# Top-k attention and a gated network on one core: bounds and epsilon moved from ScalarE to VectorE

## The chip, the core and the metric

The kernel runs on one core of a Trainium2 chip. Its time is the device time of one execution in microseconds (us); a kernel's time is the median of its runs. The core has five engines that run side by side and wait for each other through semaphores: TensorE (PE; its weight loads are listed as PEld), VectorE (DVE), ScalarE (ACT), GpSimd (POOL) and SyncE (SP), which here only issues transfers. [...]

## The reference, cut to what matters

Two stages follow each other. First attention over 8 batches of 8 heads with 576 positions of 64 values, in which each row keeps only its 32 largest scores; then a network with a gate on the 4608 x 512 result.

```python
scores = scale * np.matmul(q, k.transpose(0, 1, 3, 2))        # scale = 1/8
kth = np.partition(scores, -top_k, axis=-1)[..., -top_k:-top_k + 1]   # top_k = 32
mask = scores >= kth
scores = np.where(mask, scores, -1000000000.0)
scores = scores - np.max(scores, axis=-1, keepdims=True)
attn = np.exp(scores)
attn = attn / (np.sum(attn, axis=-1, keepdims=True) + 1e-09)
x = np.matmul(attn, v)          # then (B,H,S,D) -> (B*S, H*D) = 4608 x 512
h = x @ w_in                    # 512 x 2048
g = h * np.cos(h)
return g @ w_out                # 2048 x 512
```

Two numbers per row are needed between the scores and the exponential: the 32nd largest score, for the mask, and the largest, for the shift. They are called the bounds here. The epsilon is the 1e-09 that is added to the row's sum. The weights w_in and w_out arrive as 64-bit floats and are put together from two 32-bit words each on the core.

## The kernel before, in words

**Units and slots.** A unit is one pair of heads for one block of 128 tokens; there are 36 blocks times 4 pairs, 144 units. The main loop (L853) goes through slots. In slot i VectorE searches the largest scores of unit `u` = i, ScalarE masks and exponentiates unit `w` = i - 1, GpSimd packs unit `x` = i - 2 for the transpose, and TensorE, in every even slot, multiplies the two units `z` (i - 4 and i - 3) by the values. Between these pieces `feed` places matmuls of the network: `ff1` (L497, h) and `ff2` (L572, the output). There are three kinds of slots: `early_slot` for the first nine (i up to EARLY = 8), where weights are still loaded and transposes are done by TensorE; `slot` for the 132 in the middle (9 to 140), where the weights go through GpSimd's packing and a transposing transfer; and `last_slot`. In some of the middle slots (the first ones) weights are still decoded. All orders are written out by hand in these three functions; no scheduler changes them.

**The search on folded halves.** The 576 scores of a row are folded into two halves of 288: `rest` holds the larger of each pair (`fold_high`, L242, VectorE, one input in PSUM, the matmuls' accumulator memory, and one in SBUF, the main on-chip memory), `low` the lesser. The lesser is made on GpSimd as sum minus larger, on integers: `fold_sum` (L252) and then `fold_low` (L261). `low` has one buffer, so L252 of a unit waits until VectorE has ended the last search on the `low` of the unit before. The searches themselves are rounds of MAX8 (L323) and MATCH_REPLACE8 (L326), four rounds on `rest` and two on `low`. `merge_first` (L311) and `merge_second` (L316) join both lists to the 32nd largest; they run one slot later, around that slot's L242.

**Bounds, mask, exponential.** `bounds` turns the two ends of the list into `nb` (both times -1/8; L333) and, for each of the two heads, `nd` (the difference of the two bounds; L336), on ScalarE. `mask` (L345) and `exponentials` (L353), also on ScalarE, use them; the exponential also leaves the row sums in `den`, to which L358 adds the epsilon. `reciprocal` (L362, VectorE) follows at the head of the next slot.

**GpSimd in a middle slot.** In order: L252 (`fold_sum` of u), L379 and L381 (`split`: the words of x and its reciprocal in halves for the transfer), L261 (`fold_low`), then parts of the network: the gate's product (L559), or conversion and difference (L533, L542).

**VectorE in a middle slot.** In order: reciprocal L362, L311, L242, L316, all searches, and in even slots at the end two products that scale the values (`scale_values`, L451, two inputs in SBUF); these stand just ahead of the next slot's reciprocal.

**Weights.** `decode_first` (ScalarE) turns the high words into floats (L130) and rounds the low words to integers (L133); `decode_second` (VectorE) shifts the high part (L141); `decode_third` (GpSimd) adds the two (L151). 32 chunks of 128 x 512 go this way.

Of the kernel before, what the change touches and what calls it, by code (L numbers as in the profile page):

```python
# [10 lines left out]
F32 = mybir.dt.float32  # L11
I32 = mybir.dt.int32
U32 = mybir.dt.uint32
U16 = mybir.dt.uint16
AF = mybir.ActivationFunctionType
ALU = mybir.AluOpType

P = 128
TOPK = 32
NEG = -3.4028234663852886e38  # L20
EPS = 1e-9
# [9 lines left out]
def kernel(  # L31
# [9 lines left out]
    nc = tc.nc  # L41
    ctx.enter_context(tc.manual_schedule())
    B, H, D, S = qT.shape
# [6 lines left out]
    HS = S // 2  # L50
    SCALE = 1.0 / math.sqrt(D)
# [3 lines left out]
    consts = ctx.enter_context(tc.tile_pool(name="consts", bufs=1))  # L55
# [10 lines left out]
    nc.vector.memset(halfpi, math.pi / 2.0)  # L66
    quarter = consts.tile([P, 1], F32, tag="quarter")
    nc.vector.memset(quarter, 0.25)
    eps = consts.tile([P, 1], F32, tag="eps")
    nc.vector.memset(eps, EPS)  # L70

# [50 lines left out]
    def decode_first(n):  # L124


        for _ in range(min(n, len(wq["loaded"]))):
            st, w = wq["loaded"].popleft()
            lo, hi = st[:, :, 0], st[:, :, 1]
            nc.scalar.activation(  # L130
                out=w, in_=hi.bitcast(F32), func=AF.Prelu, scale=2.0**-111, alpha=2.0**32
            )
            nc.scalar.mul(out=lo, in_=lo.bitcast(U32), mul=2.0**-29)  # L133
            wq["second"].append((st, w))

    def decode_second(n):

        for _ in range(min(n, len(wq["second"]))):
            st, w = wq["second"].popleft()
            wi = w.bitcast(I32)  # L140
            nc.vector.tensor_scalar(  # L141
                out=wi, in0=wi, scalar1=3, scalar2=None, op0=ALU.logical_shift_left
            )
            wq["third"].append((st, w))
# [92 lines left out]

    def fold_high(u):

        s, sc = u["s"], u.pop("sc")  # L240
        u["rest"] = work.tile([P, 2, S], F32, tag="rest", name="rest", bufs=1)
        nc.vector.tensor_tensor(  # L242
            out=u["rest"][:, :, HS:S], in0=sc[:, :, 0:HS], in1=s[:, :, HS:S], op=ALU.max
        )

    def fold_sum(u):

        if not u["folds"]:
            return
        s = u["s"].bitcast(I32)  # L250
        u["low"] = work.tile([P, 2, HS], F32, tag="low", name="low", bufs=1)
        nc.gpsimd.tensor_tensor(  # L252
            out=u["low"].bitcast(I32), in0=s[:, :, 0:HS], in1=s[:, :, HS:S], op=ALU.add
        )

    def fold_low(u):

        if not u["folds"]:
            return
        low = u["low"].bitcast(I32)  # L260
        nc.gpsimd.tensor_tensor(  # L261
            out=low, in0=low, in1=u["rest"][:, :, HS:S].bitcast(I32), op=ALU.subtract
        )
# [9 lines left out]
    def topk_first(u, w):  # L273

        u["top"] = tops[u["n"] % len(tops)]
        merges = w and w["folds"]
        if merges:
            merge_first(w)
        if u["folds"]:
            fold_sum(u)  # L280
            fold_high(u)
            if u["n"] <= EARLY:
                fold_low(u)
        else:
            u["rest"] = work.tile([P, 2, S], F32, tag="rest", name="rest", bufs=1)
        if merges:
            merge_second(w)
        topk_round(u, 0)

    def topk_round(u, rnd):  # L290
# [24 lines left out]
    def merge_second(u):  # L315
        nc.vector.tensor_reduce(  # L316
            out=u["top"][:, :, TOPK - 1, 1], in_=u.pop("lesser"), axis=mybir.AxisListType.X,
            op=ALU.max,
        )
# [8 lines left out]
    def bounds(u):  # L328

        ends = u.pop("top").rearrange("p j r i -> p j (r i)")  # L330
        ends = ends[:, :, 2 * TOPK - 2 :] if u["folds"] else ends[:, :, 2 * TOPK - 2 :: 2 - 2 * TOPK]
        nb = u["nb"] = small.tile([P, 2, 2], F32, tag="nb", name="nb")
        nc.scalar.mul(out=nb, in_=ends, mul=-SCALE)  # L333
        nd = u["nd"] = small.tile([P, 2], F32, tag="nd", name="nd")
        for j in range(2):
            nc.scalar.activation(  # L336
                out=nd[:, j : j + 1], in_=ends[:, j, 1:2], func=AF.Identity,
                bias=nb[:, j, 0:1], scale=SCALE,
            )

    def mask(u):

# [6 lines left out]
    def exponentials(u):  # L349
        s, nd = u["s"], u.pop("nd")  # L350
        den = u["den"] = small.tile([P, 2], F32, tag="den", name="den")
        for j in range(2):
            nc.scalar.activation(  # L353
                out=s[:, j], in_=s[:, j], func=AF.Exp, bias=nd[:, j : j + 1], scale=1.0,
                accum_out=den[:, j : j + 1],
            )

        nc.scalar.activation(out=den, in_=den, func=AF.Identity, bias=eps, scale=1.0)  # L358

    def reciprocal(u):  # L360
        u["rden"] = small.tile([P, 2], F32, tag="rden", name="rden")
        nc.vector.reciprocal(u["rden"], u.pop("den"))  # L362

    def normalise(u):
        s, rden = u["s"], u.pop("rden")
# [266 lines left out]
    EARLY, LAST = 2 * NP, NU - NP  # L632
# [26 lines left out]
    def early_slot(i, u, w):  # L659
        n = 3 if i < 6 else 2  # L660
        topk_first(u, w)
        if i == 0:
            decode_second(1)
        scores(units[i + 1])
        for load, b, hp in at_slot.get(i, []):
            load(b, hp)
        load_weights(n)
        if w:
            bounds(w)
            mask(w)  # L670
            exponentials(w)
        topk_round(u, 1)

        decode_second(n)
        if w:
            reciprocal(w)
        topk_round(u, 2)
        topk_round(u, 3)
        if w:
            normalise(w)  # L680
        take_banks()
        take_scores(units[i + 1])
        gate(1)
        decode_third()
        feed(2)
        reduce_first()
        reduce_second()
        if i != NP:
            decode_first(n - 1)
        if w:  # L690
            transposes_now(w)
        feed(1)
        decode_first(n - len(wq["second"]))
        if w:
            values([w])
            take_values([w])
        feed(2)
        sines(2)
# [7 lines left out]
    def slot(i, u, w, x, z):  # L706
        if x:
            reciprocal(x)
        if u:
            topk_first(u, w)  # L710
            decode_second(2)
        if x:
            send(x)
        if u:
            fold_low(u)
            topk_round(u, 1)
            topk_round(u, 2)
            topk_round(u, 3)
        made = scored.get(i, [])
        if z:  # L720
            take_banks()
        feed(1)

        ahead = i < EARLY + 5 * NP
        if z and not ahead:
            values(z)
        for m in made:
            scores(m)
        if z and ahead:
            values(z)  # L730


        late = len(made) > 0

        decoding = i < EARLY + 8
        if i % 2 and not decoding:
            sines(1)
        if w:
            bounds(w)
            mask(w)  # L740
        take_banks()
        if w and late:
            exponentials(w)
        if z and not ahead:
            take_values(z)
        take_scores(units[i + 1])
        if z and ahead:
            take_values(z)
        if z:
            scale_values(z)  # L750
        if w and not late:
            exponentials(w)
        load_weights(2)
        for load, b, hp in at_slot.get(i, []):
            load(b, hp)
        gate(1)
        feed(1 if len(made) == 2 else 2)
        take_banks()
        decode_third()
        decode_first(2)  # L760
        reduce_first()
        reduce_second()
        feed(1 if len(made) == 2 else 3)
        if decoding or i == LAST:
            sines(1)

    def last_slot(i, u, w, x, z):
        if x:
            reciprocal(x)
        if u:  # L770
            topk_first(u, w)
            fold_low(u)
            topk_round(u, 1)
        bounds(w)
        mask(w)
        exponentials(w)
        take_banks()
        sines(1)
        if z:
            values(z)  # L780
        if i + 1 < NU:
            scores(units[i + 1])
        if z:
            take_values(z)
            scale_values(z)
        if i + 1 < NU:
            take_scores(units[i + 1])
        if x:
            send(x)
        reciprocal(w)  # L790
        normalise(w)
        if u:
            topk_round(u, 2)
            topk_round(u, 3)
        gate(2)
        feed(2)
        transposes_now(w)
        take_banks()
        reduce_first()
        reduce_second()  # L800
        feed(1)
        values([w])
        take_values([w])
        feed(2)
# [71 lines left out]
```

## Time and profile before

| | |
|---|---|
| time, median of 3 runs | 1498.96 us (1487.91 to 1499.81) |
| span of the profiled run | 1491.0 us |
| TensorE busy | 1409.2 us, 95% of the span |
| VectorE busy | 1332.0 us, 89% |
| ScalarE busy | 1217.2 us, 82% |
| GpSimd busy | 1165.1 us, 78% |
| `nb` L333, x144 | 199 ns each |
| `nd` L336, x288 | 287 ns each |
| epsilon L358, x144 | 296 ns each |
| low words L133, x32 | 679 ns each |
| L252 and L261, x142 each | 1439 and 1417 ns each |
| L379, x132 | 2107 ns each |

Busy time is the time in which an engine had at least one instruction in work; overlapping instructions of one engine count once. A row of the timeline gives start and duration in us from the span's start, the engine, the line, the operation, output and inputs; in brackets stands how long the engine was idle before it and what ended that wait. The chain of waits is followed back from the last instruction to what released each one, and says which engine's work the end of the kernel hangs on. The table by stages gives the busy time of each engine in a stretch, with the number of instructions in parentheses.

### The profile page before, as it was taken

To read this page: it belongs to the slowest core of one execution; us is meant where nothing else is said; L and a number is where in the kernel's file an instruction comes from. 1 tells how busy PE (TensorE), PEld (TensorE's weight loads), DVE (VectorE), ACT (ScalarE), POOL (GpSimd) and SP (SyncE) were. 2 spreads that over 40 slices of the span, in tenths; PEclk is the share of its full clock that TensorE was granted. 3 is DMA by queue.
4 is the path that set the end of the run, shared out by engine and by line. 5 is a ranking of instruction groups with operands and counts; after the bars stand their busy time and mean duration, and the time that the engine had idled before them with its cause. 6 is when DMAs were issued, how large, how long until landed. Compare 5 with 4: busy or idle time off the path is not lost.

```text
span 1491.0 us, 30595 instructions
## 1 busy us (share of the span) xinstructions
PE 1409.2 (95%) x10360; PEld 1013.3 (68%) x10360; DVE 1332.0 (89%) x4764; ACT 1217.2 (82%) x2438; POOL 1165.1 (78%) x822
## 2 busy tenths in 40 slices
PE   5678599999999999999999999999999999999998
PEld 3456366777777777777767777677667777777665
DVE  6888899999999999999999999999999999999721
ACT  6887778888888888888888888888888888888651
POOL 5688777888888888888888888888888888888410
PEclk9888799999999999999999999999999999999999
DMA  8523476656665566556655566656765566555200
GB/s 265 159 86 101 138 203 160 156 146 187 190 165 149 149 176 192 160 151 193 180 165 149 149 179 175 171 149 160 198 170 146 149 165 181 160 147 148 70 8 15
DMA packets 405549, 229.54 MB, mean 154 GB/s; under 512 B 355088, under 2 KB 371728, under 8 KB 405392
## 3 DMA queue, kind: packets, MB, share of 16 engines
q1 hardware_dynamic: 399984, 217.93, 53.8%
q10 hardware_dynamic: 5408, 9.65, 1.8%
q8 instruction: 82, 1.34, 0.4%
q14 instruction: 75, 0.61, 0.1%
HBM read 45.09 MB, written 95.94 MB: 95 GB/s over the span
## 4 chain that ended last, share of the span: by engine, by line
PE 76%; ACT 12%; DVE 5%; DMA 4%; issue 1%; POOL 0%; SPq 0%; ACTq 0%; POOLq 0%
PE mm L497 29%; PE o L572 28%; PE rim L432 10%; PE sc L223 7%; DMA pT<-rows 2%; ACT s L353 2%; DVE top L323 2%; PE rim L223 2%; ACT s L345 2%; ACT s L233 1%; DVE rest L326 1%; ACT L353 1%; ACT L552 1%; ACT x L552 1%; DVE xT L451 1%
## 5 line engine op out<-in xcount | busy, mean ns | idle before, releaser
L497 PEld LDWEIGHTS mm<-xT,w_in 128*128 128x128 f32 x4608 | 538.2, 192 | 74.5 <-issue 51.4
L572 PE MATMUL o<-w_out,g 128*128 128x512 f32 x1152 | 540.4, 603 | 17.2 <-POOL w_out L151 13.6
L497 PE MATMUL mm<-xT,w_in 128*128 128x128 f32 x4608 | 542.1, 276 | 6.2 <-DVE xT L451 2.8
L323 DVE MAX8 top<-rest 128x8 f32<-128x288 f32 x1148 | 470.3, 451 | 0.0
L326 DVE MATCH_REPLACE8 rest<-top,rest 128x288 f32<-128x288 f32 (+1 forms) x860 | 376.3, 445 | 0.0
L252 POOL TENSOR_TENSOR low<-s 128x576 int32<-128x576 int32 x142 | 204.4, 1439 | 197.5 <-DVE top L323 81.1
L572 PEld LDWEIGHTS o<-w_out,g 128*128 128x128 f32 x1152 | 203.1, 191 | 205.0 <-issue 181.3
L379 POOL COPY halves<-s 128x2304 uint16<-128x2304 uint16 x132 | 278.1, 2107 | 0.5 <-DMA rows<-halves 0.5
L353 ACT ACTIVATE s<-s,nd 128x576 f32<-128x576 f32 x288 | 220.3, 766 | 14.0 <-ACT ob L582 13.2
L323 DVE MAX8 top<-low 128x8 f32<-128x288 f32 x568 | 229.1, 445 | 0.0
L345 ACT ACTIVATE s<-s,nb 128x576 f32<-128x576 f32 x288 | 205.3, 760 | 0.0
L261 POOL TENSOR_TENSOR low<-low,rest 128x576 int32<-128x576 int32 x142 | 201.2, 1417 | 1.8 <-DVE top L316 0.9
L432 PEld LDWEIGHTS rim<-pT,v 128*64 128x64 f32 x2560 | 135.0, 141 | 66.3 <-ACT nb L333 43.2
L432 PE MATMUL rim<-pT,v 128*64 128x128 f32 (+1 forms) x2560 | 163.9, 273 | 16.4 <-ACT pT L413 8.4
L511 ACT ACTIVATE g<-mm 128x512 f32<-128x512 f32 x144 | 84.6, 588 | 114.5 <-PE mm L497 114.5
L559 POOL TENSOR_TENSOR g<-g,x 128x1024 f32<-128x1024 f32 x68 | 160.7, 2363 | 8.2 <-ACT x L552 8.2
L542 POOL TENSOR_TENSOR x<-g,x 128x1024 f32<-128x1024 f32 x68 | 160.8, 2365 | 5.7
L223 PE MATMUL sc<-k,q 64*128 64x448 f32 (+1 forms) x640 | 155.0, 594 | 7.5 <-DVE rest L326 5.5
L233 ACT COPY s<-sc 128x896 f32<-128x896 f32 x144 | 129.8, 901 | 3.2 <-PE sc L223 3.2
L326 DVE MATCH_REPLACE8 low<-top,low 128x288 f32<-128x288 f32 x284 | 123.5, 441 | 0.0
L242 DVE TENSOR_TENSOR rest<-sc,s 128x576 f32<-128x576 f32 x142 | 106.1, 747 | 11.4 <-ACT s L234 11.4
L223 PEld LDWEIGHTS rim<-k,q 64*128 64x128 f32 (+1 forms) x640 | 59.6, 184 | 56.7 <-issue 53.4
(56 smaller groups left out, 1394.3 us busy)
## 6 DMA issues: line engine op xcount, KB each, us to landing
rows<-halves SPq DMA_DIRECT2D x132, 640.0 KB, 3.0
out_dram<-ob ACTq DMA_DIRECT2D x36, 256.0 KB, 2.1
q<-in_q_dram SPq DMA_DIRECT2D x31, 288.0 KB, 3.5
st<-in_moe_w_in_dram SPq DMA_DIRECT2D x16, 512.0 KB, 5.7
v<-in_v_dram SPq DMA_DIRECT2D x32, 256.0 KB, 3.1
st<-in_moe_w_out_dram SPq DMA_DIRECT2D x16, 512.0 KB, 4.1
k<-in_k_dram SPq DMA_DIRECT2D x31, 144.0 KB, 3.7
k<-in_k_dram SPq DMA_DIRECT2D x32, 128.0 KB, 3.6
```

The costliest lines, as they stand in the source:

```text
L223: nc.tensor.matmul(to[r0 : r0 + rows, j, 0 : k1 - k0], st["q"][d, q0 : q0 + rows], st["k"][d, k0:k1], start=True, stop=True,)
L252: nc.gpsimd.tensor_tensor(out=u["low"].bitcast(I32), in0=s[:, :, 0:HS], in1=s[:, :, HS:S], op=ALU.add)
L261: nc.gpsimd.tensor_tensor(out=low, in0=low, in1=u["rest"][:, :, HS:S].bitcast(I32), op=ALU.subtract)
L323: nc.vector.max(to[:, j], src[:, j])
L326: nc.vector.match_replace(rest[:, j], to[:, j], src[:, j], NEG)
L345: nc.scalar.activation(out=s[:, j], in_=s[:, j], func=AF.Prelu, bias=nb[:, j, 1:2], scale=SCALE, alpha=FAR)
L353: nc.scalar.activation(out=s[:, j], in_=s[:, j], func=AF.Exp, bias=nd[:, j : j + 1], scale=1.0, accum_out=den[:, j : j + 1],)
L379: nc.gpsimd.tensor_copy(out=halves[:, :, 0 : 2 * S], in_=s.rearrange("p (k h) -> p h k", h=2))
L432: nc.tensor.matmul(o[d, to], lhsT, rhs, start=c == 0, stop=c == NT)
L497: nc.tensor.matmul(mm[:, at : at + w], w_in[f // FC][:, c, (f % FC) * P : (f % FC + 1) * P], blk["xT"][:, c], start=c == 0, stop=c == NC - 1,)
L542: nc.gpsimd.tensor_tensor(out=x, in0=g, in1=x, op=ALU.subtract)
L572: nc.tensor.matmul(o, g[:, at : at + P], w_out[f], start=f == 0, stop=f == NF - 1)
```

## The change

Four things move. First, `nb` and `nd` are computed by VectorE (one instruction each per unit, 128 x 4 and 128 x 2), directly behind `merge_second` at the head of the next slot; `nd` has two inputs in SBUF. Second, the epsilon is added by VectorE just ahead of the reciprocal. Third, the low words of the weights are rounded by GpSimd instead of ScalarE. Fourth, in the first nine units the lesser scores come from one VectorE minimum (`fold_now`, one input in PSUM) and not from L252 and L261 on GpSimd. It is meant to shorten ScalarE's turn in every slot, to make the mask wait for fewer handovers, and to lighten GpSimd in the first slots.

```diff
     def decode_first(n):
...
-            nc.scalar.mul(out=lo, in_=lo.bitcast(U32), mul=2.0**-29)
     def decode_second(n):
...
+            nc.gpsimd.tensor_scalar(
+                out=lo, in0=lo.bitcast(U32), scalar1=2.0**-29, scalar2=1.0, op0=ALU.mult, op1=ALU.mult
+            )
...
+    def fold_now(u):
+
+        s, sc = u["s"], u.pop("sc")
+        u["low"] = work.tile([P, 2, HS], F32, tag="low", name="low", bufs=1)
+        nc.vector.tensor_tensor(
+            out=u["low"], in0=sc[:, :, 0:HS], in1=s[:, :, HS:S], op=ALU.min
+        )
...
         if u["folds"]:
-            fold_sum(u)
+            if u["n"] > EARLY:
+                fold_sum(u)
             fold_high(u)
-            if u["n"] <= EARLY:
-                fold_low(u)
...
         if merges:
             merge_second(w)
+        if w:
+            bounds(w)
+        if u["folds"] and u["n"] <= EARLY:
+            fold_now(u)
         topk_round(u, 0)
...
-        nc.scalar.mul(out=nb, in_=ends, mul=-SCALE)
+        nc.vector.tensor_scalar(out=nb, in0=ends, scalar1=-SCALE, scalar2=None, op0=ALU.mult)
         nd = u["nd"] = small.tile([P, 2], F32, tag="nd", name="nd")
-        for j in range(2):
-            nc.scalar.activation(
-                out=nd[:, j : j + 1], in_=ends[:, j, 1:2], func=AF.Identity,
-                bias=nb[:, j, 0:1], scale=SCALE,
-            )
+        nc.vector.scalar_tensor_tensor(
+            out=nd, in0=ends[:, :, 1], scalar=SCALE, in1=nb[:, :, 0], op0=ALU.mult, op1=ALU.add
+        )
...
-        nc.scalar.activation(out=den, in_=den, func=AF.Identity, bias=eps, scale=1.0)
     def reciprocal(u):
         u["rden"] = small.tile([P, 2], F32, tag="rden", name="rden")
-        nc.vector.reciprocal(u["rden"], u.pop("den"))
+        den = u.pop("den")
+        nc.vector.tensor_scalar(out=den, in0=den, scalar1=EPS, scalar2=None, op0=ALU.add)
+        nc.vector.reciprocal(u["rden"], den)
```

The calls of `bounds` in `early_slot` and `slot`, ahead of `mask`, are taken out.

More of the change, by code (lines that the diff above doesn't have):

```diff
@@ L68 @@
     nc.vector.memset(quarter, 0.25)
-    eps = consts.tile([P, 1], F32, tag="eps")
-    nc.vector.memset(eps, EPS)
     DECODE = moe_w_in.dtype != F32
@@ L128, in decode_first @@
             st, w = wq["loaded"].popleft()
-            lo, hi = st[:, :, 0], st[:, :, 1]
+            hi = st[:, :, 1]
             nc.scalar.activation(
@@ L139, in decode_second @@
             st, w = wq["second"].popleft()
-            wi = w.bitcast(I32)
+            wi, lo = w.bitcast(I32), st[:, :, 0]
+            nc.gpsimd.tensor_scalar(
+                out=lo, in0=lo.bitcast(U32), scalar1=2.0**-29, scalar2=1.0, op0=ALU.mult, op1=ALU.mult
+            )
             nc.vector.tensor_scalar(
@@ L238, in fold_high @@
     def fold_high(u):
-        s, sc = u["s"], u.pop("sc")
+        s, sc = u["s"], u["sc"]
+        if u["n"] > EARLY:
+            del u["sc"]
         u["rest"] = work.tile([P, 2, S], F32, tag="rest", name="rest", bufs=1)
@@ L279, in topk_first @@
         if u["folds"]:
-            fold_sum(u)
+            if u["n"] > EARLY:
+                fold_sum(u)
             fold_high(u)
-            if u["n"] <= EARLY:
-                fold_low(u)
         else:
@@ L668, in early_slot @@
         if w:
-            bounds(w)
             mask(w)
@@ L738, in slot @@
         if w:
-            bounds(w)
             mask(w)
@@ L773, in last_slot @@
             topk_round(u, 1)
-        bounds(w)
+        if not u:
+            bounds(w)
         mask(w)
```

## The prediction

> **What bounds the kernel now.** I read the page from the chain down, then the stages, then single slots on VectorE and GpSimd. The chain says TensorE:
>
> ```profile
> PE 76%; ACT 12%; DVE 5%; DMA 4%; issue 1%; POOL 0%; SPq 0%; ACTq 0%; POOLq 0%
> ```
>
> Two rows of the chain in order of time show the beat: the same 32 matmuls return after 680.73 - 662.04 = 18.69 us, and 18.69 us is two slots (two head pairs). From 200 to 1400 us TensorE is busy 98 to 100 of every 100 us.
>
> ```profile
> 662.04 3.57 PE mm L497 x32
> ...
> 680.73 3.57 PE mm L497 x32
> ```
>
> VectorE is close behind. This stretch of the table by stages (columns after the window: PE, PEld, DVE, ACT, POOL busy and counts, clock, DMA) has it busy 95.9 of 100 us, GpSimd 85.7:
>
> ```profile
> 640.00:740.00 100.00, 99.84 (x725) 72.45 (x722) 95.88 (x354) 87.11 (x176) 85.69 (x58) 1.00 0.63 172
> ```
>
> One slot's turn on VectorE shows how little is left. These rows of the timeline (start, duration, engine, line, operation) begin a slot without an xT product; the slot before ended its last search (two MAX8 on `low`) at 652.01:
>
> ```profile
> 652.76 0.17 DVE L362 RECIPROCAL rden<-den 128x2 f32<-128x2 f32 x1 [0.75 <-ACT den L358]
> 652.84 0.20 DVE L311 TENSOR_REDUCE top<-top 128x34 f32<-128x68 f32 x1
> 652.96 0.75 DVE L242 TENSOR_TENSOR rest<-sc,s 128x576 f32<-128x576 f32 x1
> 653.63 0.18 DVE L316 TENSOR_REDUCE top<-top 128x2 f32<-128x34 f32 x1
> ```
>
> The 0.75 us is VectorE's only gap in two slots. L242 starts follow each other by 9.57 us (643.39 to 652.96, this gap in it) and 9.12 us; in places where nothing holds VectorE they are 8.79 us (with the xT products 9.12). So VectorE's own work is 8.79 + 9.12 = 17.91 us per pair of slots against TensorE's 18.69: 0.78 us of slack. What GpSimd does in the same moment decides this case:
>
> ```profile
> 652.18 1.41 POOL L252 TENSOR_TENSOR low<-s 128x576 int32<-128x576 int32 x1 [1.54 <-DVE top L323]
> 653.54 2.10 POOL L379 COPY halves<-s 128x2304 uint16<-128x2304 uint16 x1
> 655.58 0.40 POOL L381 COPY halves<-rden 128x256 uint16<-128x256 uint16 x1
> 655.94 1.42 POOL L261 TENSOR_TENSOR low<-low,rest 128x576 int32<-128x576 int32 x1
> ```
>
> L252 starts when the last search on `low` ends (0.17 us after it), and L379 follows with no gap. GpSimd is busy for 3.5 us at the head of every slot, exactly where the change puts its new VectorE instructions. And the trace has VectorE instructions that met such work:
>
> ```profile
> 224.79 3.43 DVE L451 TENSOR_TENSOR xT<-xT,pT 128x128 f32<-128x128 f32 x2 [2.97 <-ACT xT L439]
> ...
> 224.56 1.40 POOL L252 TENSOR_TENSOR low<-s 128x576 int32<-128x576 int32 x1 [2.72 <-ACT s L234]
> 225.91 2.17 POOL L379 COPY halves<-s 128x2304 uint16<-128x2304 uint16 x1
> ...
> 94.77 2.12 DVE L141 TENSOR_SCALAR w_out<-w_out 128x512 int32<-128x512 int32 x2
> ```
>
> The two xT products took 3.43 us in place of the usual 0.47: the first ended 0.15 us after L252, the second 0.14 us after L379. The median of L451 is 281 ns, its longest 2185. The two shifts L141 took 2.12 us, where a pair elsewhere takes 0.76. Each held L451 ends 0.14 to 0.15 us after a GpSimd instruction's recorded end, each held L141 0.28 to 0.29 us: in both cases its own duration less 0.13 us. L242 ran beside L252 in every slot and kept 740 to 759 ns.
>
> [...] L451 (two SBUF inputs) and L141 (512 elements in 415 ns[...]) wait, while L242, with one input in PSUM, does not. [...] No instruction of the trace before is a small tensor_scalar, so for `nb` and the epsilon this is unmeasured here. [...] In the changed program `nb`, `nd` and the reciprocal each wait for VectorE's own semaphore, so none starts before its predecessor's recorded end.
>
> **The change, part by part.**
> *Taken from ScalarE:* 144 `nb` (199 ns), 288 `nd` (287 ns, pairs in 0.48 us), 144 epsilons (296 ns), about 0.97 us per slot, and 32 low words (679 ns). In the middle this is worth nothing: ScalarE is busy 87 of 100 us and TensorE's 18.69 us hide it.
>
> *Added to VectorE:* per slot `nb`, `nd`, epsilon, each about 0.16 us (reciprocal 160, L316 179 ns, equally small). Without any lock that is 3 x 0.16 less some overlap, 0.5 us per slot: 17.91 + 1.0 = 18.9 us per pair, a draw with TensorE.
>
> *Their wait on GpSimd, slot without xT.* Let T be where VectorE is free (0.08 us before the last MAX8's recorded end, as all followers of MAX8 start). Epsilon takes T to T+0.16, before L252 begins at T+0.25. Reciprocal T+0.16, L316 0.87 later, over at T+1.21: `nb` asks in the middle of L252, which ends T+1.66. `nb` ends at 1.66 - 0.13 + 0.16 = T+1.69. `nd` must wait for `nb`, and L379 stands ready, as it did between the two L451, so it goes first: it ends about T+3.75, and `nd` at T+3.78. MAX8 starts about T+3.70; before it was T+0.98 (652.76 to 653.74). Cost 2.7 us. Behind `nd` all the searches stand in line, and ScalarE's mask.
> *Slot with xT.* The two xT run at T and T+0.19 ahead of L252 (their usual place, the first 0.23 us before L252: 661.50 and 661.73). The epsilon, at T+0.33, meets L252 and ends T+1.76. Reciprocal, L311, L242, L316 bring `nb` to T+2.8, inside L379, which ends T+3.75. `nb` ends T+3.78, L381 slips in (0.40), `nd` ends about T+4.15, MAX8 T+4.1 in place of T+1.37. Cost 2.7 us.
> Pair of slots: 17.91 + 2 x 2.7 = 23.3 us; VectorE becomes the bound. The 132 middle slots run now from 113.2 to 1383.6 us (L242 starts), 19.25 us a pair, start-up stalls included. 66 x (23.3 - 19.25) = +267 us. About half of the start-up stalls (11 slots at 11.3 us where 9.4 is usual, 20 us) stays: +10.
>
> *First nine slots.* GpSimd loses L252 and L261 (2.86 us a slot) and gains two or three low-word products. None is in the trace; bounds are 0.55 us (half of L533's 1051 for 1024 elements) and 1.3 us (L151's two-input form); I take 0.7, near L367's 750 ns for 576[...]. They lie beside VectorE's searches. VectorE gains fold_now (0.75, as L242, with one PSUM input so no lock), 0.5 for the small three, and about 1.5 where `nb` and `nd` meet two of these products: +2.75. It loses its waits for `den` (1.1, 1.9, 3.2 us in three slots), for ScalarE is 3 us shorter. Net +0.7 a slot, +7 us. The last four slots: nothing, since TensorE's tail covers 1400 to 1491.
>
> Sum: 1499 + 267 + 10 + 7, about 1785 us.
>
> **The rivals.**
> *Only `nd` takes the lock*[...]. Without xT: `nd` asks at T+1.36, ends T+1.68, +0.65. With xT it asks at T+1.68, a tie with L379: +0.4 or +2.4. Pair 18.9 or 20.9 us: 1500 to 1625. [...] Against: L141 is the same operation and is held.
> *No small instruction waits, faster.* 18.9 us a pair, hidden by TensorE; ScalarE's 3 us per early slot come off the first nine, perhaps 1.5 us each: 1485. For it: VectorE's 0.78 us of slack and the early waits for `den`. Against: the L451 pairs.
> *Worse collisions.* `nd` loses to L261 as well (1.4 us per pair, +94), or TensorE, with pauses, gets a lower clock as in slices of the page's first 200 us (7 or 8 tenths): about 1880.
>
> **How the numbers follow.** Lock on all three 0.72, on `nd` alone 0.14 (half of it at the tie's cheap side), none 0.09, worse 0.05. The range 1600 to 1880 takes in the main case, the dear half of the second and the near end of the last. Faster by over 1% is part of the no-lock case, 0.05; within 1% the rest of it and the cheap tie in part, 0.09; slower 0.86.
>
> **What would show it.** Right: `nb` and `nd` rows with means near 1 to 2 us, ends 0.03 us after L252 and L379; L242 to L242 at 11.5 to 12 us; the chain of waits led by VectorE, TensorE near 80%; ScalarE waiting for `nb` or `nd`. Wrong: `nb`, `nd` near 0.16 us and the beat still 18.7 us (no lock), or only `nd` long. The sum fails most easily if the order at a lock's release differs from the two L451 pairs I took it from, or if L379 moves behind `nd`.

## The result and the profile after

The changed kernel takes 1765.9 us (median of 4 runs, 1762.6 to 1767.4) against 1497.6 us: ratio 1.180, 95% interval 1.175 to 1.186. It is slower by 268 us.

TensorE has lost the lead. The chain of waits of the changed kernel, by engine and then by line (line numbers are the changed kernel's from here on; its L262, L391, L393, L271 are L252, L379, L381, L261 of before):

```profile
DVE 86%; PE 7%; ACT 2%; issue 2%; DMA 2%; SPq 0%; POOL 0%; ACTq 0%; DVEq 0%; POOLq 0%
DVE top L336 32%; DVE rest L339 19%; DVE nd L348 8%; DVE low L339 6%; DVE nb L346 5%; DVE rest L244 5%; DVE den L373 5%; PE mm L509 3%; PE o L584 3%; DVE xT L463 2%; DVE top L324 1%; DMA v<-in_v_dram 1%; DVE rden L374 1%; DVE top L329 1%; PE rim L444 1%
```

Of the span, 18% now hangs on `nd`, `nb` and the epsilon, three instructions on two or four numbers per partition. Their rows in the costliest groups (busy us, mean ns, idle before):

```profile
L348 DVE SCALAR_TENSOR_TENSOR nd<-top,nb 128x2 f32<-128x2 f32 x144 | 153.1, 1064 | 5.0
...
L373 DVE TENSOR_SCALAR den<-den 128x2 f32<-128x2 f32 x144 | 100.0, 695 | 9.0 <-ACT s L364 9.0
L346 DVE TENSOR_SCALAR nb<-top 128x4 f32<-128x4 f32 x144 | 99.0, 688 | 5.0
```

Together 352 us. At the 0.16 us that `nd` takes in the first slots, where nothing holds it, the 432 of them would be 69 us. The 283 us between (an estimate) are waiting that the profile counts as busy time of these instructions. So VectorE looks full, here from 640 to 740 us, while TensorE and the other two have time over (PE, PEld, DVE, ACT, POOL, then the granted clock):

```profile
640.00:740.00 100.00, 89.85 (x685) 64.84 (x685) 99.14 (x315) 65.05 (x109) 67.50 (x47) 0.95 0.52 146
```

What the three wait for is seen by laying VectorE's rows beside GpSimd's. First the head of a slot without xT, on VectorE:

```profile
715.93 0.15 DVE L373 TENSOR_SCALAR den<-den 128x2 f32<-128x2 f32 x1
716.12 0.17 DVE L374 RECIPROCAL rden<-den 128x2 f32<-128x2 f32 x1
716.20 0.20 DVE L324 TENSOR_REDUCE top<-top 128x34 f32<-128x68 f32 x1
716.33 0.75 DVE L244 TENSOR_TENSOR rest<-sc,s 128x576 f32<-128x576 f32 x1
716.99 0.18 DVE L329 TENSOR_REDUCE top<-top 128x2 f32<-128x34 f32 x1
717.20 0.42 DVE L346 TENSOR_SCALAR nb<-top 128x4 f32<-128x4 f32 x1
717.66 2.00 DVE L348 SCALAR_TENSOR_TENSOR nd<-top,nb 128x2 f32<-128x2 f32 x1
```

and on GpSimd:

```profile
716.19 1.40 POOL L262 TENSOR_TENSOR low<-s 128x576 int32<-128x576 int32 x1 [4.23 <-DVE den L373]
717.53 2.11 POOL L391 COPY halves<-s 128x2304 uint16<-128x2304 uint16 x1
719.58 0.41 POOL L393 COPY halves<-rden 128x256 uint16<-128x256 uint16 x1
```

L262 ends at 717.59 and `nb` at 717.62; L391 ends at 719.64 and `nd` at 719.66. The reductions and L244 between them ran beside L262 at their usual length (0.20, 0.18 and 0.75 us; 0.204, 0.179 and 0.747 on average in the kernel before). In the slot with xT just before it, the epsilon and `nb` are the held ones:

```profile
704.13 0.47 DVE L463 TENSOR_TENSOR xT<-xT,pT 128x128 f32<-128x128 f32 x2
704.52 1.37 DVE L373 TENSOR_SCALAR den<-den 128x2 f32<-128x2 f32 x1
...
707.01 0.93 DVE L346 TENSOR_SCALAR nb<-top 128x4 f32<-128x4 f32 x1
707.97 0.29 DVE L348 SCALAR_TENSOR_TENSOR nd<-top,nb 128x2 f32<-128x2 f32 x1
```

```profile
704.35 1.52 POOL L262 TENSOR_TENSOR low<-s 128x576 int32<-128x576 int32 x1 [2.74 <-DVE top L336]
705.82 2.10 POOL L391 COPY halves<-s 128x2304 uint16<-128x2304 uint16 x1
707.86 0.40 POOL L393 COPY halves<-rden 128x256 uint16<-128x256 uint16 x1
```

The epsilon ends 0.02 us after L262, `nb` 0.02 us after L391, `nd` with L393. L244 starts at 706.13, 716.33 and 729.34: 23.21 us for two slots, where before it was 18.69.

The other engines wait for VectorE. ScalarE's mask (L356) waits 372.5 us for the bounds and TensorE's first layer (L509) 127.4 us for xT. Neither is a cost of its own: L356 is not among the lines that the chain names, and L509 has 3% of it. Their rows:

```profile
L509 PE MATMUL mm<-xT,w_in 128*128 128x128 f32 x4608 | 627.6, 300 | 178.4 <-DVE xT L463 127.4 <-ACT x L525 49.1 <-ACT ob L594 1.8
...
L356 ACT ACTIVATE s<-s,nb 128x576 f32<-128x576 f32 x288 | 207.4, 768 | 372.9 <-DVE nb L346 372.5
```

### The profile page after: what moved, and what is told of

It is laid out like the page before. It is cut to its first block, busy times and chain, and to the rows that moved or that the text cites. A ratio compares the mean times of both kernels' runs of the same rounds, so it can differ in the third digit from the quotient of the medians.

```text
span 1764.8 us, 30625 instructions
## 1 busy us (share of the span) xinstructions
PE 1501.6 (85%) x10360; PEld 1089.1 (62%) x10360; DVE 1670.5 (95%) x5204; ACT 1086.0 (62%) x1830; POOL 1162.5 (66%) x836
## 4 chain that ended last, share of the span: by engine, by line
DVE 86%; PE 7%; ACT 2%; issue 2%; DMA 2%; SPq 0%; POOL 0%; ACTq 0%; DVEq 0%; POOLq 0%
DVE top L336 32%; DVE rest L339 19%; DVE nd L348 8%; DVE low L339 6%; DVE nb L346 5%; DVE rest L244 5%; DVE den L373 5%; PE mm L509 3%; PE o L584 3%; DVE xT L463 2%; DVE top L324 1%; DMA v<-in_v_dram 1%; DVE rden L374 1%; DVE top L329 1%; PE rim L444 1%
## 5 line engine op out<-in xcount | busy, mean ns | idle before, releaser
L509 PE MATMUL mm<-xT,w_in 128*128 128x128 f32 x4608 | 627.6, 300 | 178.4 <-DVE xT L463 127.4
L509 PEld LDWEIGHTS mm<-xT,w_in 128*128 128x128 f32 x4608 | 612.7, 215 | 262.0 <-DVE xT L463 133.5
L584 PE MATMUL o<-w_out,g 128*128 128x512 f32 x1152 | 540.6, 603 | 19.4 <-POOL w_out L151 16.5
L262 POOL TENSOR_TENSOR low<-s 128x576 int32<-128x576 int32 x133 | 194.4, 1462 | 453.2 <-DVE den L373 265.6
L356 ACT ACTIVATE s<-s,nb 128x576 f32<-128x576 f32 x288 | 207.4, 768 | 372.9 <-DVE nb L346 372.5
L391 POOL COPY halves<-s 128x2304 uint16<-128x2304 uint16 x132 | 278.1, 2107 | 0.2
L271 POOL TENSOR_TENSOR low<-low,rest 128x576 int32<-128x576 int32 x133 | 187.6, 1411 | 1.2 <-DVE top L329 1.2
L223 PE MATMUL sc<-k,q 64*128 64x448 f32 (+1 forms) x640 | 158.8, 590 | 12.8 <-DMA k<-in_k_dram 11.2
L571 POOL TENSOR_TENSOR g<-g,x 128x1024 f32<-128x1024 f32 x68 | 160.6, 2362 | 2.5 <-ACT x L564 1.9
L348 DVE SCALAR_TENSOR_TENSOR nd<-top,nb 128x2 f32<-128x2 f32 x144 | 153.1, 1064 | 5.0
L244 DVE TENSOR_TENSOR rest<-sc,s 128x576 f32<-128x576 f32 x142 | 106.2, 748 | 6.2 <-ACT s L234 6.2
```

What stands on the lines that cost most here:

```text
L244: nc.vector.tensor_tensor(out=u["rest"][:, :, HS:S], in0=sc[:, :, 0:HS], in1=s[:, :, HS:S], op=ALU.max)
L262: nc.gpsimd.tensor_tensor(out=u["low"].bitcast(I32), in0=s[:, :, 0:HS], in1=s[:, :, HS:S], op=ALU.add)
L271: nc.gpsimd.tensor_tensor(out=low, in0=low, in1=u["rest"][:, :, HS:S].bitcast(I32), op=ALU.subtract)
L348: nc.vector.scalar_tensor_tensor(out=nd, in0=ends[:, :, 1], scalar=SCALE, in1=nb[:, :, 0], op0=ALU.mult, op1=ALU.add)
L356: nc.scalar.activation(out=s[:, j], in_=s[:, j], func=AF.Prelu, bias=nb[:, j, 1:2], scale=SCALE, alpha=FAR)
L391: nc.gpsimd.tensor_copy(out=halves[:, :, 0 : 2 * S], in_=s.rearrange("p (k h) -> p h k", h=2))
```

## The experiments

The theory, drawn from the rows above: a small instruction of two or four elements on VectorE is held until the GpSimd instruction at work has ended, and at the head of each slot these are L262 and L391 (`nb` ended 0.03 us after L262, `nd` 0.02 us after L391). This wait is what the prediction calls a lock. The rivals: it is the number of dependent instructions on VectorE; it is ScalarE's later mask; it is the low words or fold_now. Six runs undo or reshape one part each; two more use the finding on other instructions.

**Epsilon alone on VectorE.** `bounds` is as before and is called ahead of `mask` again.

```diff
-        if w:
-            bounds(w)
...
-        nc.vector.tensor_scalar(out=nb, in0=ends, scalar1=-SCALE, scalar2=None, op0=ALU.mult)
+        nc.scalar.mul(out=nb, in_=ends, mul=-SCALE)
...
```

> Epsilon stays on VectorE, the bounds go back to ScalarE; low words and fold_now as in the change. [...] in slots with xT the epsilon (asked 0.33 us after VectorE is free) waits for L252 and costs 1.4 us; in slots without xT it is over before L252 begins and costs 0.2. Pair of slots 17.91 + 1.6 = 19.5 us against 18.95 before: about 1525 us. Rival, every added instruction on VectorE costs the same share of the 268 us: one of three, about 1590. Rival, it is the later mask that costs (ScalarE waits for VectorE's bounds): 1500 or less.

Measured: 1542.2 us, ratio 1.033 (1.029 to 1.037). The usual beat is 10.56 + 8.92 = 19.48 us a pair, the 19.5 expected if the epsilon waits for L262. The total lies 17 us above the expected one, and 11 us in the profiled run (1536.0). Past the start-up that run's middle has 10 us over its usual pairs. Most of it stands in eight slots without xT of about 10.46 us (six shorter slots with xT take a part back). In each of the eight VectorE waited 0.43 to 0.83 us for ScalarE's row sums, and the epsilon, now late, met L262 and took 0.76 to 1.17 us where 0.16 is usual without xT. That a third of the loss falls to each instruction (1590) is out, and so is the mask as the cause of these 49 us (1500 or less).

**Bounds alone on VectorE.** The epsilon is ScalarE's again.

```diff
...
+        nc.scalar.activation(out=den, in_=den, func=AF.Identity, bias=eps, scale=1.0)
...
-        nc.vector.tensor_scalar(out=den, in0=den, scalar1=EPS, scalar2=None, op0=ALU.add)
         nc.vector.reciprocal(u["rden"], den)
```

> Bounds on VectorE, epsilon back on ScalarE; low words and fold_now as in the change. [...] nb waits for L252, nd for L379, whatever came before, so the searches begin at L379's end nearly as in the change: pair about 22.9 us, about 1755 us. So the two halves do not add up (1525 and 1755 against 1766). Rival, cost by number of instructions: two thirds of 268 us, about 1675.

Measured: 1748.9 us, ratio 1.171 (1.166 to 1.175), beat 11.73 + 11.13 = 22.86 us. Alone the epsilon costs 49 us and the bounds 256 us (against 1493.3 us of the kernel before, measured beside them); both together cost 268. They do not add up because in each slot the searches start when GpSimd's big copy is over, whichever of the three has waited for L262. (In the change's slots with xT they start when the short copy behind it, L393, is over: 23.21 us a pair there, 0.35 us more than here.) Two slots on VectorE show it, one without and one with xT; `nd` ends 0.02 us after GpSimd's big copy in both (that ends at 713.80 and 725.27):

```profile
711.23 0.55 DVE L348 TENSOR_SCALAR nb<-top 128x4 f32<-128x4 f32 x1
711.82 2.00 DVE L350 SCALAR_TENSOR_TENSOR nd<-top,nb 128x2 f32<-128x2 f32 x1
...
722.95 0.30 DVE L348 TENSOR_SCALAR nb<-top 128x4 f32<-128x4 f32 x1
723.29 2.00 DVE L350 SCALAR_TENSOR_TENSOR nd<-top,nb 128x2 f32<-128x2 f32 x1
```

**Neither.** Both on ScalarE; the low words on GpSimd and fold_now are left. The edit is the two above together:

```diff
-        nc.vector.tensor_scalar(out=nb, in0=ends, scalar1=-SCALE, scalar2=None, op0=ALU.mult)
+        nc.scalar.mul(out=nb, in_=ends, mul=-SCALE)
...
-        nc.vector.tensor_scalar(out=den, in0=den, scalar1=EPS, scalar2=None, op0=ALU.add)
...
```

> Only the low words on GpSimd and fold_now on VectorE are left of the change; bounds and epsilon as before. [...] the middle slots beat as before (18.7 us a pair), the first nine differ by a few us: 1490 to 1505. Rival, the weights' low words or fold_now carry a part of the loss: 1520 or more.

Measured: 1492.95 us, ratio 1.0001 (0.9989 to 1.0013). These two parts of the change together gain or cost nothing that can be seen.

**The same values in one-element instructions.** Everything stays on VectorE, in eight instructions in place of three:

```diff
-        nc.vector.tensor_scalar(out=nb, in0=ends, scalar1=-SCALE, scalar2=None, op0=ALU.mult)
+        for j in range(2):
+            for e in range(2):
+                nc.vector.tensor_scalar(
+                    out=nb[:, j, e : e + 1], in0=ends[:, j, e : e + 1],
+                    scalar1=-SCALE, scalar2=None, op0=ALU.mult,
+                )
...
-        nc.vector.scalar_tensor_tensor(
-            out=nd, in0=ends[:, :, 1], scalar=SCALE, in1=nb[:, :, 0], op0=ALU.mult, op1=ALU.add
-        )
+        for j in range(2):
+            nc.vector.tensor_scalar(
+                out=nd[:, j : j + 1], in0=ends[:, j, 1:2], scalar1=SCALE,
+                scalar2=nb[:, j, 0:1], op0=ALU.mult, op1=ALU.add,
+            )
```

and the epsilon likewise, once per head.

> All on VectorE as in the change, same values, but nb, nd and epsilon as eight instructions of one element per partition with one tensor input (nd takes nb as a per-partition scalar) in place of three of two or four elements. [...] none waits for GpSimd: rows near 0.1 to 0.2 us each, pair about 19.4 us, about 1525 us. Rival, number of dependent instructions on VectorE: 8 in place of 3, slower than the change, about 1850. [...] about 1766 or more, with rows that end at L252's and L379's ends.

Measured: 1526.2 us, ratio 1.023 (1.020 to 1.026); beat 9.90 + 9.50 = 19.40 us. More instructions, 240 us less. This run decides against the number of instructions, and against the later mask: here too ScalarE gets its bounds from VectorE. The groups (1152 instructions, 134 us busy):

```profile
L348 DVE TENSOR_SCALAR nb<-top 128x1 f32<-128x1 f32 x576 | 56.6, 146 | 0.0
...
L354 DVE TENSOR_SCALAR nd<-top,nb 128x1 f32<-128x1 f32 x288 | 46.8, 204 | 0.0
...
L381 DVE TENSOR_SCALAR den<-den 128x1 f32<-128x1 f32 x288 | 30.2, 143 | 8.6 <-ACT s L371 8.6
```

None of them is held (the longest takes 207 ns), though GpSimd is at the same place: the four `nb` at 707.98 took 0.40 us in all beside an L262 from 707.04 to 708.45. What is left over 1493 is VectorE's own work, 19.40 against TensorE's 18.69 us a pair.

**nd alone in its two-input form.** The bounds on VectorE, `nb` in one-element form, the epsilon on ScalarE; `nd` is left as the change has it.

```diff
-        nc.vector.tensor_scalar(out=nb, in0=ends, scalar1=-SCALE, scalar2=None, op0=ALU.mult)
+        for j in range(2):
+            for e in range(2):
+                nc.vector.tensor_scalar(
+                    out=nb[:, j, e : e + 1], in0=ends[:, j, e : e + 1],
+                    scalar1=-SCALE, scalar2=None, op0=ALU.mult,
+                )
         nd = u["nd"] = small.tile([P, 2], F32, tag="nd", name="nd")
         nc.vector.scalar_tensor_tensor(
...
```

> As the run with the bounds alone on VectorE, but nb as four one-element instructions[...]. [...] in slots without xT nd ends with L252 (+0.6 us), in slots with xT it is ready when L252 ends and loses to L379 (+2.4): pair 20.9 us, about 1625 us. If a two-element two-input instruction does not wait: nd 0.2 us, pair about 19.1, about 1510.

Measured: 1620.3 us, ratio 1.082 (1.081 to 1.085), beat 9.68 + 11.13 = 20.81 us. The two-input instruction of two elements is held (2.09 us below) like the xT products of 128 (2.185 at the longest in the kernel before). VectorE in a slot with xT, then GpSimd in the same slot:

```profile
710.64 0.38 DVE L350 TENSOR_SCALAR nb<-top 128x1 f32<-128x1 f32 x4
711.00 2.09 DVE L355 SCALAR_TENSOR_TENSOR nd<-top,nb 128x2 f32<-128x2 f32 x1
```

```profile
709.51 1.52 POOL L264 TENSOR_TENSOR low<-s 128x576 int32<-128x576 int32 x1 [0.71 <-DVE top L338]
710.98 2.10 POOL L398 COPY halves<-s 128x2304 uint16<-128x2304 uint16 x1
```

`nd` asked 0.02 us after L398's start and had to sit it out; it ended at 713.09, L398 at 713.08. In slots without xT it asks earlier, inside L264, and takes 0.30 us.

**GpSimd's side: fold_now in every slot.** The whole change, and the lesser scores made on VectorE throughout; L262 and L271 are gone from GpSimd.

```diff
...
-            if u["n"] > EARLY:
-                fold_sum(u)
             fold_high(u)
...
-        if u["folds"] and u["n"] <= EARLY:
+        if u["folds"]:
             fold_now(u)
...
-            fold_low(u)
...
```

> The whole change, and fold_now in every slot that folds: VectorE gets 0.75 us more work per slot (133 slots, 100 us in all), GpSimd loses L252 and L261 (L262 and L271 in the change's numbers). [...] VectorE's own work is then 17.9 + 1.0 + 1.5 = 20.4 us a pair; with L252 gone from the head of the slot, L379 can run before the slot begins, at least in slots with xT, and the small instructions meet less: 20.4 to 22.4 us a pair, 1590 to 1720 us, so faster than the change with more work on the bounding engine. Rival, VectorE is long because of the work given to it, whatever GpSimd does: 1766 + 100, about 1865 us.

Measured: 1748.9 us, ratio 1.169 (1.167 to 1.171). The range expected was missed. That VectorE's own work sets the time is refuted (1865 expected): with 100 us more of it the kernel is 17 us faster, and the two intervals do not meet. But the small instructions found other GpSimd work to wait for: a pair of slots took about 22.8 us where the work alone had been put at 20.4. On VectorE and GpSimd in a slot with xT:

```profile
711.90 0.15 DVE L369 TENSOR_SCALAR den<-den 128x2 f32<-128x2 f32 x1
...
713.23 1.88 DVE L342 TENSOR_SCALAR nb<-top 128x4 f32<-128x4 f32 x1
715.15 0.16 DVE L344 SCALAR_TENSOR_TENSOR nd<-top,nb 128x2 f32<-128x2 f32 x1
```

```profile
712.38 0.40 POOL L389 COPY halves<-rden 128x256 uint16<-128x256 uint16 x1 [4.24 <-DVE rden L370]
712.74 2.35 POOL L567 TENSOR_TENSOR g<-g,x 128x1024 f32<-128x1024 f32 x1
```

The big copy had indeed run before the slot, as expected, and the epsilon is free. But L389 waits for the reciprocal at the slot's head, and the gate's product L567, whose cosine ScalarE had ready at 709.76, is queued behind it; it starts 0.49 us ahead of `nb`, which ends 0.02 us after it. I had looked at what leaves the head of the slot and not at what moves up.

**The other use of the finding.** In the kernel before, xT products that came late were held in the same way (3.43 us for two, usually 0.47). With the first input read from PSUM they have one SBUF input, and ScalarE's copy falls away:

```diff
-        nc.scalar.copy(out=to, in_=room[0][:, 0 : n * P])
+        if not us[0]["paired"]:
+            nc.scalar.copy(out=to, in_=room[0][:, 0 : n * P])
...
-        for u in us:
+        for i, u in enumerate(us):
             to = block_of[u["tok"]]["xT"][:, u["hp"]]
-            nc.vector.tensor_tensor(out=to, in0=to, in1=u.pop("pT")[:, 2 * NT + 1], op=ALU.mult)
+            nc.vector.tensor_tensor(
+                out=to, in0=room[0][:, i * P : (i + 1) * P], in1=u.pop("pT")[:, 2 * NT + 1], op=ALU.mult
+            )
```

> Kernel before, but the xT product of the middle slots reads its first input straight from PSUM (ScalarE's copy of it to SBUF is left out), so that it has one SBUF input. [...] no L451 is ever held (longest about 0.4 us, before 2.185), the two start-up slots that took 18.8 and 15.1 us lose 3 us or more each; the middle is bound by TensorE and keeps its beat: 1485 to 1492 in place of about 1495. Rival, these waits are hidden: no change within 0.2%.

Measured, on the kernel before: 1482.0 us, ratio 0.991 (0.989 to 0.993), a little more than expected. The longest product is 292 ns (2185 before):

```profile
L452 DVE TENSOR_TENSOR xT<-rim,pT x132: 262/278/292, 164.4 to 1393.7; 128x128 f32<-128x128 f32 x132
```

The two start-up slots went from 18.8 and 15.1 to 15.6 and 11.9 us; the last slot's L242 starts 9.0 us earlier. In the kernel before, six of the 132 products began inside L252 or L379 and all six were held; here eleven began inside L252, with 1.24 us or more of it to come, and none was. The edit takes away the wait for ScalarE's copy as well, so the gain in time does not come from the missing hold alone. The same edit on the run with neither bounds nor epsilon on VectorE:

> The run without bounds and epsilon on VectorE (low words on GpSimd and fold_now kept), with the xT product read from PSUM as in the other run of this call: the same gain on that base, 1483 to 1490, perhaps the fastest of all; if the first slots hide nothing, 1493.

Measured, with the low words and fold_now kept: 1483.3 us, ratio 0.992 (0.990 to 0.993). The same, within the intervals; these two versions beat both kernels, the one before by 0.8 to 0.9%.

## Why the prediction was right

*Mechanism.* All three small instructions are held by GpSimd, the tensor_scalars of two and four elements too: the epsilon, 128x2, took 1.37 us beside L262 (704.52), `nb`, 128x4, 0.93 us beside L391 (707.01). The trace before has no tensor_scalar so small; it had L141, the same operation on 512 elements, and did not show whether small ones wait as well. That one element is not held was found only in the run of one-element instructions (207 ns at the longest); why it is not was not shown. In the slot without xT each started after the recorded end of the one that it reads, as predicted (the reciprocal 0.04 us after the epsilon, `nb` 0.03 us after L329, `nd` 0.04 us after `nb`).

*Slot without xT.* With T at 715.93: `nb` ended at T+1.69 (T+1.69 predicted), `nd` at T+3.73 (3.78), the searches began at T+3.65 (3.70). *Slot with xT.* With T at 704.13: epsilon T+1.76 (1.76), `nb` T+3.81 (3.78), `nd` T+4.13 (4.15), searches T+4.06 (4.1). The order at the release, which I had named as the weakest point, was as in the xT pairs of before: the held instruction goes in between, its dependent one loses to GpSimd's next.

*Sum.* Pair 23.21 us (23.3). Middle 1542.7 against 1270.5 us, from the first L244 of the middle to the one that follows its last slot: +272 (+267 and +10 predicted). Half of the start-up stalls stayed: 1542.7 less 66 x 23.21 is 11 us (10); the prediction gave no working for this half, so that term was lucky. The end was unchanged, as predicted (107.3 us from the last slot's L244 to the end, 107.4 before).

*Mis-sized.* The first nine slots cost +1.9 us (107.6 against 105.7), not +7. The new VectorE instructions took 16.1 us there, not 9 x 2.75 = 24.8: only `nb` met GpSimd (6.8 us in eight slots), while `nd` took 0.16 us each. The waits for `den` fell from 11.5 to 1.8 us; the predicted net of +0.7 a slot comes out only if the three waits that it names, 2.1 us on average, stand for all nine slots. The weights' shifts (L141), no longer held (429 ns at the longest, 1621 before), took 3.3 us less, which was not in the sum. A low word on GpSimd took 657 ns (0.7 taken). Without held instructions these slots gain: 102.6 us in the run of one-element instructions.

*Signs.* The beat I gave, "11.5 to 12 us" from L242 to L242, came as 13.02 and 10.19: with xT the epsilon's wait lies ahead of that instruction and is counted to the slot before. The mean of `nb`, 688 ns, lies below the 1 to 2 us given as a sign, though it fits the slots as worked out (0.5 and 1.0 us). TensorE's share is 85%, not near 80: its matmuls took longer, as said below. The 0.5 us a slot without a wait was put as three times 0.16 less some overlap; there is none: after the epsilon at 715.93 the reciprocal starts 0.19 us later. ScalarE did lose about 131 us of busy time (1217 to 1086) and nothing came of it, as predicted.

*Rivals.* That `nd` alone waits would have been 1500 to 1625; the run built that way, with the epsilon left on ScalarE, measured 1620, so the dear side of that estimate was right and its cause was not the kernel's. No wait at all would have been 1485; the run without held instructions measured 1526, with VectorE at 19.4 us a pair against TensorE's 18.7. It has eight instructions where this rival has three, so the 1485 itself was not tested.

## What to carry to other kernels

Before small arithmetic is moved to VectorE, look at what GpSimd runs at that moment. In these traces a two-input product or sum with both inputs in SBUF (128 and 2 elements per partition: xT up to 2.185 us where 0.281 is the median, `nd` up to 2.002 where 0.160 is the least) and a tensor_scalar in SBUF with 2, 4 or 512 elements (epsilon up to 1.390 us, `nb` up to 2.014, L141 in the kernel before up to 1.700; the least 0.139, 0.170 and 0.414) waited for the GpSimd instruction at work, and a dependent pair could wait for two (`nb` to 717.62 for L262, `nd` to 719.66 for L391). The reductions, the reciprocal and the searches, also on SBUF data, ran beside GpSimd at their usual length (all 144 reciprocals of the changed kernel took 165 to 168 ns, L329 177 to 190; two MAX8 took 0.81 us at 709.76, beside L571). The cost was set by GpSimd's list, not by the instruction's size (0.16 to 2.00 us for the same `nd`), and it hides as busy time: a row of two elements with a mean of 1 us is the sign. One element per instruction (207 ns at the longest), or an input in PSUM (xT 292 ns at the longest), avoided the wait; taking L262 and L271 away from GpSimd mostly moved the next ones up (1748.9 against 1765.9 us).

## What was not expected of the hardware

GpSimd is slowed as well, which the prediction had left out of its sum: L262 took 1.52 us when the two xT products stood just ahead of it and 1.40 us otherwise. With the products read from PSUM, all 142 of these instructions took about 1.4 us (mean 1.409, 1.439 in the kernel before). And TensorE's granted clock fell to 0.95 in the middle (0.918 over the span, 0.981 before) once it had pauses of some 10%; its matmuls (L509) took 300 ns in place of 276. The other long runs had a lower clock too (0.946 at 1620 us, 0.921 and 0.923 at 1749 us). Whether the pauses brought the clock down was not tested.
